# Turning B and C of two more pairs of chunks by VectorE: a state-space scan and an MLP on one core

## The chip, the core and the metric

The kernel runs on one core of a Trainium2 chip. A core has a matrix engine (TensorE, PE in the profile; PEld is its weight load), three engines for elementwise work (VectorE, DVE; ScalarE, ACT; GpSimd, POOL) and SyncE (SP), which here only issues transfers. Each engine works through its own queue of instructions in order and waits on semaphores for the others. Sixteen DMA engines move data between the memory (HBM) and the core's own memory (SBUF); TensorE writes its results to eight banks of PSUM. The metric is the device time of one execution in microseconds.

## The reference

Two blocks follow each other, all in float32 but for the weights, which arrive as float64.

The first is a state-space layer over 4 batches, 8 heads and 768 tokens, with a head width of 32 and a state width of 16. Per batch and head, in chunks of tokens:

```python
cum = cumsum(log(clip(a)))                       # inside the chunk
M = (C @ B.T) * exp(cum_i - cum_j) * causal      # tokens by tokens
y = M @ x + (C @ state) * exp(cum_i)
state = exp(cum_last) * state + (B * exp(cum_last - cum_j)).T @ x
```

The second is an MLP on the result, laid out as 3072 tokens by 256 (8 heads by 32):

```python
h = x @ w_in                                     # 256 -> 2048
g = maximum(h, 0) + alpha * minimum(h, 0)        # alpha per hidden unit
out = g @ w_out                                  # 2048 -> 256
```

## The kernel before

**Chunks, pairs, groups.** The kernel takes chunks of 128 tokens, 24 in all. Two neighbouring chunks of a batch are a pair (`gp`, 0 to 11); two pairs are a group of 512 tokens (0 to 5). A pair's state-space work gives 256 columns of xT, the input of the MLP in transposed form. While TensorE does the MLP of one group, the pairs of the next group are worked in between.

**Order.** There is no scheduler: the order of the program is the order on each engine. `first_two` does pairs 0 and 1. The loop `for f in range(FIRST, NF)` near the end does the MLP of group 0 (16 slices of 128 hidden units, steps 4 to 15 here) and spreads pairs 2 and 3 over it. From there on the loop over `quad` does the five other groups, in products of half the size combined as in Strassen's method, with the remaining pairs between them.

**A pair.** `load_pair` issues its transfers on SyncE's queue, `pair_loads` scales B with GpSimd (`bn`, line 533), and the generator `pair` does the rest in stages, each run by one call of `ssm`:
1. B and C of the pair are needed with the state's width on the partitions. Either TensorE transposes them against an identity (line 669, four 128x128 blocks into a PSUM tile from `ss_tile`) and ScalarE copies the result to SBUF (`bc`, line 672), or `turn_bc` has made `bc` before, with one VectorE transpose of 32x32 blocks (line 574). For this second way the rows must lie in SBUF so that every 32x32 block holds what is to be turned; the loads of lines 210 to 217 bring them in this form, in rows of 512 bytes (8 tokens by 16 numbers).
2. The new states (lines 629, 642, 645), C spread and decayed (lines 679, 682), and VectorE's scans of the decays (line 567), which read the tiles `abc`.
3. The products of B and C (line 742), times the decays (line 753, VectorE).
4. The products that give y (lines 797 and 805), and ScalarE's copy to xT (line 817).

Which way a pair goes is set in `load_pair` by `turned = gp > GC` with `GC = 4`: pairs 5 to 11 are turned by VectorE, pairs 2, 3 and 4 by TensorE (pairs 0 and 1 have a code of their own). A turned pair still loads B in its natural form, in rows of 64 bytes, since `bn` needs it; it doesn't load C so. `load_pair(2, ...)` is called with `parted=True` inside `first_two`: it loads chunk 0 of the pair and returns two functions for chunk 1, which are called some transfers later. `load_pair(3)` is issued at step 5, `load_pair(4)` at step 10.

**PSUM tiles.** While group 0 is in work, `ss_tile` deals its tiles in turn from a ring of two (`ss`) and one more bank (`bank(2)`), by a counter that every call moves on.

**Weights.** They come as float64 in pieces of 512 KB (`raw`; w_in and w_out by turns) and are made float32 by hand: ScalarE (lines 273, 283, 286), GpSimd (line 278), VectorE (sign and shift, lines 296 and 308), GpSimd again (line 330). The table `CONVERTED` says at which step a piece is converted. Group 0's MLP in line 1095 needs w_in, line 1142 needs w_out; ScalarE and VectorE apply the slopes between them (lines 1098 and 1099), and VectorE's line 1099 is the last to read the PSUM buffer `hp`, of which there are two. Sums of weights (line 1171) and of tokens (line 1183), which the other groups need, are GpSimd's.

```python
CONVERTED = {(4, 1): ("5", 5), (5, 1): ("6", 6), (6, 1): ("7",), (7, 0): ("8", 7), (7, 1): (8,),
```

Of the kernel before, what the change touches and what calls it, by code (L numbers as in the profile page):

```python
# [9 lines left out]
F32 = mybir.dt.float32  # L10
# [12 lines left out]
def kernel(  # L23
# [25 lines left out]
    nc = tc.nc  # L49
# [4 lines left out]
    batch, H, S, D = x.shape  # L54
    N = B.shape[-1]
    P = 128
    Q = 128
# [8 lines left out]
    GC = 4  # L66
# [9 lines left out]
    NB = 2  # L76
# [15 lines left out]
    work = ctx.enter_context(tc.tile_pool(name="work", bufs=2))  # L92
# [4 lines left out]
    gp = ctx.enter_context(tc.tile_pool(name="gp", bufs=16))  # L97
# [6 lines left out]
    def bank(i):  # L104


        return ps_q.tile([P, 512], F32, name="bank", tag=f"q{i}")
# [13 lines left out]
    loads = {}  # L121

    def load_rows(i, eng=nc.sync):

        rows = ld.tile([RW, Q], F32, name="rows")
        eng.dma_start(out=rows, in_=a.rearrange("b h (c t) -> (b h c) t", t=Q)[i * RW : (i + 1) * RW])
        loads["r", i] = rows
# [3 lines left out]
    def load_a(t, b, c, eng=nc.sync):  # L131
        first = a[b, 0:1, c * Q : (c + 2) * Q]
        eng.dma_start(out=t, in_=bass.AP(tensor=first.tensor, offset=first.offset,
                                             ap=[[S, H], [0, N], [1, 2 * Q]]))
# [4 lines left out]
    def load_tokens(dst, src, t0):  # L139


        d = dst.rearrange("p j (h w) -> p j h w", h=H)
        for k in range(2):
            for j in range(2):
                t = t0 + k * Q + j * HQ
                nc.sync.dma_start(out=d[HQ * k : HQ * (k + 1), j],
                                  in_=src[:, t : t + HQ, :].rearrange("h p w -> p h w"))
# [16 lines left out]
    def load_products(gp, ap):  # L164
        b, c = divmod(2 * gp, CPB)
        rows = scratch["pf", b // 2].rearrange("(b h c) t -> b h (c t)", b=2, h=H)
        rows = rows[b % 2, :, c * Q : (c + 2) * Q]
        nc.sync.dma_start(out=ap, in_=rows.unsqueeze(1).to_broadcast([H, N, 2 * Q]))

    def load_pair(gp, decays=True, parted=False):  # L170


        b, c = divmod(2 * gp, CPB)
        turned = gp > GC
        nat = ldx.tile([P, 3, 2, H * N], F32, name="nat")
        xt = ldx.tile([P, 2, HD], F32, name="xt")

        ap = ldx.tile([P, 2 * Q], F32, name="ap")
        if gp == 0:
            load_a(ap, b, c)  # L180
        elif gp > NB:
            load_products(gp, ap)
        if gp == 0:
            load_rows(0, nc.scalar)
        abc = []
        if gp >= HALF:
            load_tokens(nat[:, 0], B[b], c * Q)
        def load_bc(k):
            ts = slice((c + k) * Q, (c + k + 1) * Q)
            for i, src in enumerate((B,) if turned else (B, C)):  # L190
                eng = nc.scalar if gp == 0 and i else nc.sync
                eng.dma_start(out=nat[:, i, k].rearrange("p (h n) -> p h n", h=H),  # L192
                              in_=src[b, :, ts, :].rearrange("h p n -> p h n"))

        def load_x(k):
            ts = slice((c + k) * Q, (c + k + 1) * Q)
            nc.sync.dma_start(out=xt[:, k].rearrange("p (h d) -> p h d", h=H),  # L197
                              in_=x[b, :, ts, :].rearrange("h p d -> p h d"))

        for k in range((1 if parted else 2) if gp < HALF else 0):  # L200
            load_bc(k)
            if gp >= NB:
                load_x(k)
        for k in range(2 if gp < NB else 0):
            load_x(k)
        if gp == 0:
            nc.scalar.dma_start(out=al_n, in_=moe_alpha.rearrange("(k p) -> k p", p=P))
            loads["a", 1] = prep.tile([P, 2 * Q], F32, name="a1")
            load_a(loads["a", 1], b, c + 2)
        for i, src in enumerate((B, C) if turned else ()):  # L210


            for e in range(2):
                first = src[b, e : e + 1, c * Q : (c + 2) * Q, :]
                nc.sync.dma_start(out=nat[:, 1 + e, i],
                                  in_=bass.AP(tensor=first.tensor, offset=first.offset,
                                              ap=[[2 * S * N, P // 32], [8 * N, 32], [1, 8 * N]]))
        for k in range(2 if gp >= NB else 0):
            abc.append(lda.tile([P, H * Q], F32, name="abc"))
        loads["p", gp] = nat, abc, xt, ap  # L220
        if gp >= HALF:
            load_tokens(xt, x[b], c * Q)
        if decays:
            for part in load_spread(gp, b, c):
                pass
        return lambda: load_bc(1), lambda: load_x(1)

    def load_second():

# [116 lines left out]
    for v in range(2):  # L346
        vs = slice(HQ * v, HQ * (v + 1))
        nc.vector.tensor_copy(out=ident_q[vs].rearrange("p (c t) -> p c t", c=4),
                              in_=ident[vs, vs].unsqueeze(1).to_broadcast([HQ, 4, HQ]))
# [171 lines left out]
    def pair_loads(gp):  # L521

        b, c = divmod(2 * gp, CPB)
        nat, abc, xt, ap = loads["p", gp]

        bn = work.tile([P, 2, H * N], F32, name="bn")
        i, bi = divmod(b, 2)
        if gp >= HALF:
            pj = prt[i].rearrange("p (j b m h) -> p j b m h", j=2, b=2, h=H)[:, :, bi, c // 2]
        else:  # L530
            pj = (prt[i if gp >= NB else "short"]
                  .rearrange("p (b h c) -> p b c h", b=2, h=H)[:, bi, c : c + 2])
        nc.gpsimd.tensor_tensor(
            out=bn.rearrange("p k (h n) -> p k h n", h=H),
            in0=nat[:, 0].rearrange("p k (h n) -> p k h n", h=H),
            in1=pj.unsqueeze(3).to_broadcast([P, 2, H, N]), op=ALU.mult)
        return bn
# [12 lines left out]
    bcs = {}  # L550
# [3 lines left out]
    def scan_half(dec, abc, k, w):  # L554
# [10 lines left out]
        for i in range(2):  # L565
# [2 lines left out]
                                         data1=ident_p[0], initial=0.0, op0=ALU.mult,  # L568
                                         op1=ALU.add)

    def turn_bc(gp):

        bcs[gp] = work.tile([P, 4, Q], F32, name="bc")
        nc.vector.transpose(
            bcs[gp].rearrange("p (i k) t -> p i (k t)", i=2)
            .rearrange("p i (c b) -> p i b c", b=8),
            loads["p", gp][0][:, 1:].rearrange("p e i (b n) -> p (i b) e n", n=N))
        decs[gp] = work.tile([P, 2, H, Q], F32, name="dec")
        scan_half(decs[gp], loads["p", gp][1], 0, 0)

    def pair(gp):

        b, c = divmod(2 * gp, CPB)
        nat, abc, xt, ap = loads["p", gp]
        last = c + 2 == CPB
        fine = gp >= 2 * GC // 2
# [75 lines left out]


        bc = bcs.pop(gp, None)
        if bc is None:
            tp = ss_tile()
            for i in range(2):
                for k in range(2):
                    nc.tensor.transpose(tp[:, (2 * i + k) * P : (2 * i + k + 1) * P],
                                        nat[:, i, k], ident)  # L670
            bc = work.tile([P, 4, Q], F32, name="bc")
            nc.scalar.copy(out=bc.rearrange("p i t -> p (i t)"), in_=tp)
# [140 lines left out]
        for w in range(KC):  # L813
            if half:
                nc.scalar.copy(out=xts[g][:, :, (q + w) * Q : (q + w + 1) * Q], in_=y[w])
            if not half:
                nc.scalar.copy(out=xts[g][:, w, q * Q : (q + 2) * Q],
                               in_=y[w].rearrange("p k t -> p (k t)"))
# [317 lines left out]
    def output(f, half=None):  # L1136

        if f == 0:
            pos[0] = [bank(i).rearrange("p (t m) -> p t m", t=2) for i in range(GC // 2)]
        gt = gts[0, f]  # L1140
        for t in range(GC) if half is None else range(2 * half, 2 * half + 2):
            nc.tensor.matmul(pos[0][t // 2][:, t % 2], gt[:, t * Q : (t + 1) * Q], w_out[:, f],  # L1142
                             start=(f == 0 and t % 2 == 0), stop=(f == NF - 1),
                             skip_group_check=True)
# [309 lines left out]
    for f in range(FIRST, NF):  # L1454
        if f in (5, 10):
            load_pair(3 + f // 10)
        if f == 5:
            load_rows(1)
        hidden(0, f)
        for part in range(2):  # L1460
            if part:
                if f <= 10:
                    ssm(2)
                if f >= 9:
                    ssm(3)
            for i in CONVERTED.get((f, part), ()):
                if isinstance(i, str):
                    convert_a(*pieces[int(i)])
                else:
                    convert_next(first=False)  # L1470
        if f == 14:
            bns[4] = pair_loads(4)
            rows_clamp(1)
            held["pr"] = rows_scan(1)
            rows_out(1)
        if f == 8:
            bns[3] = pair_loads(3)
        output(f - FIRST)
        if f in in_steps:
            weight_sums(wi, in_sums, 0, in_steps[f])  # L1480
# [99 lines left out]
```

## Time and profile before

| what | value |
|---|---|
| runs | 356.65, 356.97, 358.07 us (median 356.97) |
| span of the profiled execution | 355.9 us |
| its own device time | not given beside the span; the median of the runs lies 1.07 us above it |
| TensorE busy | 349.3 us (98%), granted clock 1.000 |
| VectorE / ScalarE / GpSimd busy | 235.8 / 171.8 / 204.4 us |
| DMA | 105581 packets, 79896 of them under 512 bytes, 30.24 MB |
| DMA share in the second to fourth slice of 40 | 0.8 to 0.9 |
| line 669, transposes of pairs 2, 3, 4 | 12, 0.27 us each, at 29.0, 51.1 and 78.0 us |
| line 574, VectorE's turns of pairs 5 to 11 | 7, 1.11 us each |

How to read it: the span runs from the first to the last instruction. An engine's line in a timeline is start, length, engine, line of the kernel, operation, what is written from what, shape and count; in brackets the idle time before it and who ended that. SPq is SyncE's queue: the time that an issue took there, and not the transfer's. Neighbouring matmuls overlap, so what one costs is read from start to start. The DMA share is the mean busy share of the sixteen engines; it can pass 1 a little, since packets overlap.

### The profile page before, as it was taken

The page shows a single profiled execution, that of the slowest core. Times are in us where ns is not written, and L with a number is a line of the kernel's source. Part 1 is how long each engine was busy: PE and PEld are TensorE (multiplying, and loading weights), DVE is VectorE, ACT ScalarE, POOL GpSimd, SP SyncE. Part 2 cuts the span into 40 slices and gives each one's busy share as a digit, 9 for nine tenths or more (in the row PEclk, how much of TensorE's full clock was granted, in tenths as well). Part 3 has the DMA queues.
Part 4 walks back from the last instruction along what each step waited for, and adds up shares of the span by engine and source line. Part 5 has one row for each costly group of instructions (what it writes and reads, how often), then busy time and mean ns, then how long its engine had stood idle before and what let it go on. Part 6 is the DMA issues. An engine that isn't in the chain of part 4 may idle for free.

```text
span 355.9 us, 7778 instructions
## 1 busy us (share of the span) xinstructions
PE 349.3 (98%) x2985; PEld 284.4 (80%) x2985; DVE 235.8 (66%) x482; ACT 171.8 (48%) x391; POOL 204.4 (57%) x228
## 2 busy tenths in 40 slices
PE   8899999999999999999999999999999999999996
PEld 4576665578788888888888888888888888888885
DVE  6876986998748756847747856757856633643363
ACT  3477576535355346345345445345445344443431
POOL 6776568589939855725646626637526535434520
PEclk9999999999999999999999999999999999999999
DMA  7899989607345403503423423422001001001102
GB/s 138 182 202 270 329 174 279 148 17 159 106 83 128 102 3 75 104 2 77 78 57 74 86 51 71 85 55 65 11 2 31 0 2 29 2 1 31 31 0 59
DMA packets 105581, 30.24 MB, mean 85 GB/s; under 512 B 79896, under 2 KB 101448, under 8 KB 105544
## 3 DMA queue, kind: packets, MB, share of 16 engines
q1 hardware_dynamic: 103048, 29.43, 36.3%
q10 hardware_dynamic: 2496, 0.32, 0.6%
q8 instruction: 23, 0.38, 0.5%
q14 instruction: 14, 0.11, 0.1%
HBM read 26.32 MB, written 3.42 MB: 84 GB/s over the span
## 4 chain that ended last, share of the span: by engine, by line
PE 89%; SPq 4%; DMA 3%; DVE 2%; ACT 1%; POOL 1%; issue 0%; DVEq 0%; ACTq 0%
PE bank L1216 33%; PE hp L1241 29%; PE bank L1142 6%; PE ss L1241 6%; PE hp L1095 3%; DMA raw<-in_moe_w_in_dram 2%; SPq L192 2%; PE ss L787 1%; PE ss L731 1%; PE hp L1110 1%; PE bank L1209 1%; PE ss L805 1%; PE ss L779 1%; DMA xt<-in_x_dram 1%; SPq L197 1%; PE ss L742 1%
## 5 line engine op out<-in xcount | busy, mean ns | idle before, releaser
L1298 POOL TENSOR_TENSOR gt<-gt 128x512 f32<-128x512 f32 x58 | 74.2, 1279 | 21.1 <-DVE gt L1226 16.3
L1216 PE MATMUL bank<-gt,w_out 128*128 128x256 f32 x320 | 83.5, 381 | 0.0
L1216 PEld LDWEIGHTS bank<-gt,w_out 128*128 128x128 f32 x320 | 60.1, 190 | 9.2 <-issue 1.0
L1288 POOL TENSOR_TENSOR gt<-gt 128x512 f32<-128x512 f32 x20 | 25.4, 1269 | 62.5 <-DVE gt L1226 49.7
L1226 DVE SCALAR_TENSOR_TENSOR gt<-hp,s_mul,gt 128x256 f32<-128x256 f32 x96 | 42.0, 479 | 29.1 <-ACT gt L1224 26.8
L1224 ACT ACTIVATE gt<-hp,s_alpha 128x256 f32<-128x256 f32 x96 | 40.3, 471 | 34.5 <-PE hp L1241 31.4
L1216 PE MATMUL bank<-gt,ws 128*128 128x256 f32 x224 | 55.9, 379 | 0.0
L1216 PEld LDWEIGHTS bank<-gt,ws 128*128 128x128 f32 x224 | 42.3, 190 | 5.6
L1241 PE MATMUL hp<-xs,w_in 128*128 128x256 f32 x160 | 41.9, 384 | 0.0
L1241 PE MATMUL hp<-xs,ws 128*128 128x256 f32 x160 | 41.1, 380 | 0.0
L1267 DVE TENSOR_TENSOR hp<-hp,u 128x512 f32<-128x512 f32 x20 | 14.0, 700 | 35.2 <-ACT u L1265 35.2
L1241 PEld LDWEIGHTS hp<-xs,ws 128*128 128x128 f32 x160 | 30.3, 190 | 4.3 <-POOL xs L1183 0.2
L1241 PEld LDWEIGHTS hp<-xs,w_in 128*128 128x128 f32 x160 | 29.7, 190 | 4.5
L1142 PE MATMUL bank<-w_out,gt 128*128 128x256 f32 x128 | 31.1, 385 | 0.4 <-POOL w_out L330 0.4
L1142 PEld LDWEIGHTS bank<-w_out,gt 128*128 128x128 f32 x128 | 23.6, 190 | 7.2 <-issue 2.9
L1241 PE MATMUL ss<-xT,w_in 128*128 128x256 f32 x96 | 24.6, 379 | 0.0
L645 POOL TENSOR_TENSOR sm<-state,bmask 128x256 f32<-128x256 f32 (+1 forms) x10 | 6.2, 620 | 29.0 <-DVE state L642 29.0
L1095 PE MATMUL hp<-xT,w_in 128*128 128x512 f32 x48 | 22.8, 596 | 0.0
L561 DVE TENSOR_TENSOR_SCAN dec<-abc,bank 128x192 f32<-128x192 f32 x48 | 22.7, 522 | 0.0
L1256 ACT COPY m<-hp 128x512 f32<-128x512 f32 x8 | 4.7, 586 | 35.7 <-PE hp L1241 35.7
L1265 ACT COPY u<-hp 128x512 f32<-128x512 f32 x20 | 11.7, 585 | 19.4 <-PE hp L1241 19.4
L1226 DVE SCALAR_TENSOR_TENSOR gt<-c,s_mul,gt 128x256 f32<-128x256 f32 x40 | 20.6, 555 | 0.0
(232 smaller groups left out, 608.2 us busy)
## 6 DMA issues: line engine op xcount, KB each, us to landing
abc<-z SPq DMA_DIRECT2D x24, 192.0 KB
raw<-in_moe_w_in_dram SPq DMA_DIRECT2D x8, 512.0 KB
raw<-in_moe_w_out_dram SPq DMA_DIRECT2D x8, 512.0 KB
abc<-z SPq DMA_DIRECT2D x8, 512.0 KB
out_dram<-o_sb SPq DMA_DIRECT2D x32, 64.0 KB
nat<-in_B_dram SPq DMA_DIRECT2D x26, 64.0 KB
xt<-in_x_dram SPq DMA_DIRECT2D x12, 128.0 KB
xt<-in_x_dram SPq DMA_DIRECT2D x24, 64.0 KB
```

Of the source, the lines that this page charges most:

```text
L192: eng.dma_start(out=nat[:, i, k].rearrange("p (h n) -> p h n", h=H), in_=src[b, :, ts, :].rearrange("h p n -> p h n"))
L561: nc.vector.tensor_tensor_scan(out=dv[:, o : o + SQ], data0=abc[k][:, s : s + SQ], data1=ident_p[0][:, :SQ], initial=0.0, op0=ALU.mult, op ...
L1095: nc.tensor.matmul(hp, w_in[:, k, f * P : (f + 1) * P], xts[g][:, k], start=(k == 0), stop=(k == KC - 1))
L1142: nc.tensor.matmul(pos[0][t // 2][:, t % 2], gt[:, t * Q : (t + 1) * Q], w_out[:, f], start=(f == 0 and t % 2 == 0), stop=(f == NF - 1), s ...
L1216: nc.tensor.matmul(ms[g][i][:, h], w, blocks[g, z][n][:, p], start=(q == 0 and h == 0), stop=(q == NQ - 1), skip_group_check=True)
L1224: nc.scalar.mul(o[:, p], h[:, p], s_alpha[:, fs[p]])
L1226: nc.vector.scalar_tensor_tensor(out=o[:, p], in0=h[:, p], scalar=s_mul[:, fs[p]], in1=o[:, p], op0=ALU.mult, op1=ALU.max)
L1241: nc.tensor.matmul(to[:, p], w(2 * z + p), b, start=start and p == 0, stop=True, skip_group_check=True)
L1265: nc.scalar.copy(out=u2, in_=A)
L1267: nc.vector.tensor_tensor(out=Y, in0=Y, in1=u2, op=ALU.add)
L1288: nc.gpsimd.tensor_tensor(out=tc_, in0=g22, in1=g12, op=ALU.subtract)
L1298: eng.tensor_tensor(out=o, in0=x0, in1=x1, op=ALU.subtract)
```

## The change

Pairs 2 and 3 are now turned by VectorE as pairs 5 to 11 are. Their C is no longer loaded in its natural form, and TensorE's eight transposes, two PSUM tiles and ScalarE's two copies go. In their place come, for each of the two pairs, four loads of 64 KB in rows of 512 bytes (two of B, two of C) and one VectorE transpose.

For pair 2 the four loads are issued with the second part of its loads, after chunk 1's B. Its turn is made in `pair`, where the transposes were, in step 4 of group 0 and ahead of the conversions of that step. For pair 3 they follow its other B and x loads, and its turn is made at step 8, one step ahead of the first stage of that pair. Pair 4 stays as it was.

```diff
-        turned = gp > GC
+        turned = gp >= NB and gp != GC
...
-        for i, src in enumerate((B, C) if turned else ()):
-            for e in range(2):
-                first = src[b, e : e + 1, c * Q : (c + 2) * Q, :]
-                nc.sync.dma_start(out=nat[:, 1 + e, i], ...)
+        def load_blocks():
+            for i, src in enumerate((B, C)):
+                for e in range(2):
+                    first = src[b, e : e + 1, c * Q : (c + 2) * Q, :]
+                    nc.sync.dma_start(out=nat[:, 1 + e, i],
+                                      in_=bass.AP(tensor=first.tensor, offset=first.offset,
+                                                  ap=[[2 * S * N, P // 32], [8 * N, 32], [1, 8 * N]]))
+        if turned and not parted:
+            load_blocks()
...
-        return lambda: load_bc(1), lambda: load_x(1)
+        return lambda: (load_bc(1), load_blocks()), lambda: load_x(1)
...
-    def turn_bc(gp):
-        bcs[gp] = work.tile([P, 4, Q], F32, name="bc")
+    def turned_bc(gp):
+        bc = work.tile([P, 4, Q], F32, name="bc")
         nc.vector.transpose(
-            bcs[gp].rearrange("p (i k) t -> p i (k t)", i=2)
+            bc.rearrange("p (i k) t -> p i (k t)", i=2)
             .rearrange("p i (c b) -> p i b c", b=8),
             loads["p", gp][0][:, 1:].rearrange("p e i (b n) -> p (i b) e n", n=N))
+        return bc
+
+    def turn_bc(gp):
+        bcs[gp] = turned_bc(gp)
...
         bc = bcs.pop(gp, None)
+        if bc is None and not fine:
+            bc = turned_bc(gp)
...
         if f == 8:
             bns[3] = pair_loads(3)
+            bcs[3] = turned_bc(3)
```

(`fine` is true from pair 4 on; `NB` is 2.)

More of the change, by code (lines that the diff above doesn't have):

```diff
@@ L209, in load_pair @@
             load_a(loads["a", 1], b, c + 2)
-        for i, src in enumerate((B, C) if turned else ()):
-            for e in range(2):
-                first = src[b, e : e + 1, c * Q : (c + 2) * Q, :]
-                nc.sync.dma_start(out=nat[:, 1 + e, i],
-                                  in_=bass.AP(tensor=first.tensor, offset=first.offset,
-                                              ap=[[2 * S * N, P // 32], [8 * N, 32], [1, 8 * N]]))
+        def load_blocks():
[7 more added lines that the diff above has]
+            load_blocks()
         for k in range(2 if gp >= NB else 0):
```

## The prediction

> **What bounds the kernel now.** I read the page's busy times first, then TensorE's waits, then the chain that ended last, then the timelines of the stretch from 16 to 80 us, where every edited instruction lies.
>
> ```profile
> PE 349.3 (98%) x2985; PEld 284.4 (80%) x2985; DVE 235.8 (66%) x482; ACT 171.8 (48%) x391; POOL 204.4 (57%) x228
> ```
>
> TensorE is busy for 349.3 of 355.9 us. Of its listed waits only one lies after 22 us: 0.4 us for GpSimd's conversion of a piece of w_out (line 330). So a microsecond taken off TensorE's queue after 22 us shortens the run, as long as the others keep up. Where they nearly don't, the chain shows:
>
> ```profile
> 29.84 7.45 DMA raw<-in_moe_w_in_dram
> ...
> 38.13 0.83 POOL wt L278
> ...
> 38.98 0.69 DVE wr L308
> ...
> 44.52 1.28 POOL w_out L330
> ...
> 45.84 0.48 PE bank L1142
> ```
>
> A raw piece of w_in (the fifth, "in4") is issued at 29.84 and lands at 37.28. Its conversion goes through ScalarE, GpSimd and VectorE (38.98), VectorE then works without a gap to 44.43, GpSimd converts the next piece to 45.79, and TensorE, idle since 45.40, goes on. Two places before it are as tight: VectorE's line 1099 of step 6 ends at 40.33 and the products of line 742 start at 40.34 (0.10 after TensorE could); step 7's ends at 43.30 and line 1095 starts at 43.45, 2.00 after the group before it, where the same pair elsewhere takes 1.83 (33.25 to 35.08): 0.17. So from 40 to 46 us TensorE is tied to the landing of in4.
>
> The four transposes that go, with their neighbours, once for pair 2 and once for pair 3:
>
> ```profile
> 27.28 1.91 PE L1095 MATMUL hp<-xT,w_in 128*128 128x512 f32 x4
> 29.02 0.60 PE L669 MATMUL ss<-ident,nat 128*128 128x128 f32 x4
> 29.46 1.89 PE L1142 MATMUL bank<-w_out,gt 128*128 128x256 f32 x8
> ...
> 51.09 0.66 PE L669 MATMUL ss<-ident,nat 128*128 128x128 f32 x4
> 51.59 1.89 PE L1142 MATMUL bank<-w_out,gt 128*128 128x256 f32 x8
> ```
>
> VectorE's queue where the two new turns go, after the first line and before the third:
>
> ```profile
> 30.59 0.75 DVE L1099 SCALAR_TENSOR_TENSOR gt<-hp,s_mul,gt 128x512 f32<-128x512 f32 x1
> 32.51 0.43 DVE L296 TENSOR_SCALAR wr<-raw 128x512 uint32<-128x512 uint32 x1 [1.17 <-DMA raw<-in_moe_w_out_dram]
> ...
> 50.31 0.75 DVE L1099 SCALAR_TENSOR_TENSOR gt<-hp,s_mul,gt 128x512 f32<-128x512 f32 x1 [0.24 <-ACT gt L1098]
> ```
>
> And SyncE's queue, where a natural load of C is followed by an issue that must wait for room:
>
> ```profile
> 16.57 0.58 SPq L192 DMA_DIRECT2D nat<-in_C_dram  x1
> 17.19 2.19 SPq L197 DMA_DIRECT2D xt<-in_x_dram  x1
> ```
>
> **The change, part by part.**
>
> *TensorE* loses 4 + 4 transposes. Start to start they cost 29.46 - 29.02 = 0.44 (line 1095 before them takes its usual 1.72 to 1.74, so I take 0.46 against a start at 29.00) and 51.59 - 51.09 = 0.50.
>
> *ScalarE* loses the copies of bc (0.61 at 30.26, 0.58 at 51.78). After the first it idles 1.71, after the second it has work that GpSimd is late for anyway: nothing.
>
> *VectorE* gains two turns. The same form runs seven times later in this trace at 1.11 us (line 574). Pair 2's comes after line 1099 ends at 31.25 and before line 296 at 32.51, where VectorE idles 1.17 for the second piece of w_out ("out1"): it fills the gap, 31.3 to 32.4. Without that gap the cost would be 1.11 on the path. Queued behind it are the sign and shift of out1 (lines 296 and 308), for which GpSimd's line 330 waits. Pair 3's comes after the shift at 49.38, so at 50.07 to 51.2. Behind it: line 1099 of step 9 (0.9 late; its buffer is next needed at 57.3), line 296, and the shift at 52.28, needed by GpSimd at 54.84. From the end of the turn to the end of that shift there are 0.66 + 0.80 + 0.69 = 2.15 us of work, so the turn must have started by 54.84 - 2.15 - 1.11 = 51.5. At 50.07 it costs nothing; the cover is 1.4 us.
>
> *Bank rotation.* Without the two tiles for the transposes every later tile of these pairs moves to another bank. Each has been read by then (pair 3's second y goes to bank 2, whose next user is at 94.7): nothing.
>
> *SyncE's queue and the transfers.* Pair 2: two C loads go (0.58 each), four block loads come (two of B 1.17, two of C 1.12, by the pair at 82 us), all before "in3"; moved back by them are in3, the store of pf, x, out1, two abc, ap and in4. Pair 3: the same, with only abc, rows and late weights behind. GpSimd's queue keeps its order and its instructions. Two ends for in4:
> - Issue alone: 2.29 - 1.16 = 1.13 us later, if SyncE's waits stay.
> - Transfers alone: from 47 to 49 us C and x move 196 KB in 1.78 us of full share, 0.89 per 1024 packets. Out go 2 x 0.89. In come 4 x 64 KB in rows of 512 bytes; the nearest row is abc, also 512 bytes, 340 GB/s at a share of 1.09 (30 to 32 us), so 0.21 each. Net 1.78 - 0.84 = 0.94 earlier.
> The second is the nearer: the engines' share is about 1 from 29 to 43 us, and SyncE spends some 5 us from 17 to 26 waiting for room (2.19, 1.63, 1.82 and 1.56 against 0.5), which swallows 1.13. Between 19 and 22 us the share is only 0.73, 0.8 us unused behind the small packets; part of it should come back. I take 1.1 for in4 and out1. The other limit is VectorE itself: its gaps from 31.3 to 38.98 are 1.17, 1.05, 0.21 and 0.50; less the 1.11 of the turn, 1.8.
>
> One rule speaks against the edit. The Trainium skill, "DMA: Bandwidth & Descriptors", section Measured, gives 0.95 us for a transfer of 64 KB whatever its rows, and calls smaller ones descriptor-dominated. It was measured on another queue, and no row here times a block load alone. By it six small loads instead of four would add 2 x 0.95 = 1.9 us, and the sum would be about 1.5 us slower than before instead of the forecast below.
>
> A second, "VectorE: DVE Perf Modes", section Rules for kernel authors, sends 128x128 transposes to TensorE if the result may lie in PSUM. In busy time it fits the rows here (0.46 to 0.50 plus a copy of 0.6, against 1.11); by it the edit is a loss of next to nothing, but it doesn't ask which engine is full.
>
> **The sum.** Write e for how much earlier VectorE's shift at 38.98 comes. TensorE's ledger is 0.46 + (0.10 + 0.17 + 0.44) = 1.17 up to 45.84, but no more than e, then 0.50 at 51.1: at most 1.67. A second chain caps it. From 49.38 GpSimd and VectorE hand the conversions to each other with hardly a gap, and at 78.55 GpSimd starts the first token sum (line 1183), which ends at 79.28; TensorE uses it at 79.35, in a group of 0.95 where its like take 0.86. That chain moves by e, plus 0.27 (VectorE's wait at 68.25 for ScalarE, which waits for TensorE) plus 0.08. After it TensorE has no wait. So the gain is the least of 1.67, e + 0.50 and e + 0.35. With e = 1.1: 1.45. The profiled span becomes 355.9 - 1.45 = 354.45; the median of the runs stands 1.07 above the span, so 356.97 - 1.45 = 355.5 us.
>
> **The rivals.**
>
> *The weights land no earlier (e about 0).* For it: in4 lands 7.4 us after its issue, far more than its own 1.3 us, so what it waits for isn't all seen. Against it: the full shares. Then the first 1.17 are gone and the second chain leaves 0.35: 356.6. With e = -1.1, the other end, 0.75 slower: 357.7.
>
> *Slower: pair 3's rows land late and VectorE stands in its turn.* Place: the turn at 50.07. It decides from a start of 51.5; each microsecond beyond delays the conversions of 54.84 by one, and through line 1183 TensorE, less 0.35. If SyncE gains nothing, the last block is issued at about 47.7 + 2.3 = 50.0; pair 1's x landed 3.3 us after its issue, so 53.3: 358.4. With in4's 7.45 it would be 57.4 and 362.5. To be 0.5% slower the turn must start after 53.6. Against it: two loads of 1024 packets, each with up to 3.89 us of issue, are gone ahead of the blocks, and SyncE comes to them earlier.
>
> *More than the ledger.* Three groups of TensorE run 0.2 long beside their like (1.93 instead of 1.73, after line 742 and the rounds of pair 2); if these were hidden waits on the same chain, 0.4 to 0.6 more: 354.9 to 355.1. Against it: the same 1.93 recurs in places with nothing late.
>
> **How the numbers follow.** A difference of 0.5%, 1.8 us, is about what measurement can tell from no change here (runs 356.65 to 358.07). Forecast 0.56, own range 355.0 to 356.1; no earlier landing 0.17; late rows 0.17; more than the ledger 0.10. Faster by over 0.5% (under 355.18): the last and a quarter of the first, 0.24. Slower (over 358.76): three quarters of the late rows, 0.13. Else 0.63. The range of 354.8 to 358.2 leaves out a twentieth below and most of the late rows above.
>
> **What would show it.** No line 669 transposes before 70 us; two more turns of 1.11, the first without a wait at about 31.3; out1 and in4 landing about 1 us earlier; line 1142 after step 8 without its 0.4; line 1183's first at about 77.1; TensorE without a new wait. I'm wrong if VectorE waits in a turn, if in4 lands at 37.3 or later, or if TensorE waits in the 70s.

## The result, and the profile after

The changed kernel takes 358.06 us in the median of 20 runs (356.15 to 360.46), the kernel before on the same chip 356.59 us (20 runs, 355.82 to 358.07). The ratio is 1.0038, with a 95% interval of 1.0024 to 1.0051: slower, by 1.5 us where 1.45 us less had been forecast. It lies inside the range given and inside the 0.5% that was called hard to tell from nothing, but on the other side, and the forecast mechanism is not what decides it.

The busy times of the changed kernel, from the first part of the page:

```profile
PE 348.8 (98%) x2977; PEld 283.6 (80%) x2977; DVE 238.2 (67%) x484; ACT 171.2 (48%) x389; POOL 203.9 (57%) x228
```

The edit is there in full: eight TensorE transposes and two ScalarE copies fewer, two VectorE turns more. (Numbers of lines have moved: 278 is now 281, 286 is 289, 296 is 299, 308 is 311, 330 is 333, 533 is 536, 574 is 577, 1095 is 1105, 1099 is 1109, 1142 is 1152, 1171 is 1181, 1183 is 1193, 1241 is 1251.)

VectorE's timeline of the changed kernel at the two turns and behind the second (start, length, engine, line, operation, operands; in brackets the idle time before it and what ended that):

```profile
29.91 0.69 DVE L311 SCALAR_TENSOR_TENSOR wr<-wt,wr 128x512 uint32<-128x512 uint32 x1 [1.06 <-POOL wt L281]
30.58 0.75 DVE L1109 SCALAR_TENSOR_TENSOR gt<-hp,s_mul,gt 128x512 f32<-128x512 f32 x1
31.25 1.11 DVE L577 STREAM_TRANSPOSE bc<-nat 128x512 f32<-128x512 f32 x1
32.21 0.42 DVE L299 TENSOR_SCALAR wr<-raw 128x512 uint32<-128x512 uint32 x1
33.13 0.69 DVE L311 SCALAR_TENSOR_TENSOR wr<-wt,wr 128x512 uint32<-128x512 uint32 x1 [0.50 <-POOL wt L281]
...
50.61 1.13 DVE L577 STREAM_TRANSPOSE bc<-nat 128x512 f32<-128x512 f32 x1 [2.01 <-DMA nat<-in_C_dram]
51.59 0.68 DVE L1109 SCALAR_TENSOR_TENSOR gt<-hp,s_mul,gt 128x512 f32<-128x512 f32 x1
52.19 0.40 DVE L299 TENSOR_SCALAR wr<-raw 128x512 uint32<-128x512 uint32 x1
52.69 0.69 DVE L311 SCALAR_TENSOR_TENSOR wr<-wt,wr 128x512 uint32<-128x512 uint32 x1
53.30 1.50 DVE L299 TENSOR_SCALAR wr<-raw 128x512 uint32<-128x512 uint32 x1
56.67 0.69 DVE L311 SCALAR_TENSOR_TENSOR wr<-wt,wr 128x512 uint32<-128x512 uint32 x1 [1.86 <-POOL wt L281]
```

Pair 2's turn runs at 31.25 without a wait, as forecast. Pair 3's has VectorE standing for 2.01 us until the last block of C lands. GpSimd in the same stretch of the changed kernel:

```profile
50.80 0.65 POOL L536 TENSOR_TENSOR bn<-nat,prt 128x256 f32<-128x256 f32 x1
52.72 1.79 POOL L1181 TENSOR_TENSOR ws<-w_in 128x512 f32<-128x512 f32 x1 [1.28 <-ACT wg L289]
54.47 1.47 POOL L333 TENSOR_TENSOR w_in<-wr,wg 128x512 uint32<-128x512 uint32 x1
```

and of the kernel before:

```profile
52.33 1.14 POOL L533 TENSOR_TENSOR bn<-nat,prt 128x256 f32<-128x256 f32 x1
53.44 1.44 POOL L1171 TENSOR_TENSOR ws<-w_in 128x512 f32<-128x512 f32 x1
54.84 1.27 POOL L330 TENSOR_TENSOR w_in<-wr,wg 128x512 uint32<-128x512 uint32 x1
```

Before, the first weight sum (line 1171) starts the moment GpSimd is free. After, GpSimd idles 1.28 us ahead of it. The view names ScalarE, but the sum writes a tile of the pool that holds the raw weights (`wld`, tag `raw`), and the last reader of the piece whose buffer it takes is VectorE's sign at 52.19. In all five profiles with a late turn (below) the sum starts 0.13 to 0.14 us after that sign ends (here 52.59 and 52.72), and in one of them (`after_look_2`) ScalarE is not named. The sum then runs beside the shift at 52.69 and the next sign, and three instructions run longer than before: the sum 1.79 for 1.44, line 333 1.47 for 1.27, and the sign 1.50 for 0.87.

What TensorE makes of it, from its timeline in the changed kernel:

```profile
44.38 1.99 PE L1152 MATMUL bank<-w_out,gt 128*128 128x256 f32 x8 [0.44 <-POOL w_out L333]
...
65.34 1.98 PE L1105 MATMUL hp<-xT,w_in 128*128 128x512 f32 x4 [1.05 <-DVE gt L1109]
```

The old wait for w_out is still there, and at step 13 there is a new one of 1.05 us, which the kernel before does not have:

```profile
65.51 1.99 PE L1095 MATMUL hp<-xT,w_in 128*128 128x512 f32 x4
```

**Reading the two traces against each other.** Three points of a profile carry all that follows: the start of step 4 (TensorE's first line 1095 with 512 columns), VectorE's third shift of that stretch, "S" (line 308 at 38.98 before, line 311 at 37.52 after), and the start of the xs product (TensorE's first product with `xs`, line 1241, 79.35 and 79.17). Behind the xs product nothing differs: it ends the span 276.4 to 276.7 us later in all profiles of this study. A run's own time lies 1.7 to 1.8 us above its span (357.36 for 355.6 here). By that distance the first profile of before, with its span of 355.9, was of a run of about 357.65, one us above that kernel's median.

### The profile page after: what moved, and what is told of

Read it like the earlier page. It is cut to its first block, busy times and chain, and to the rows that moved or that the text cites. A ratio compares the mean times of both kernels' runs of the same rounds, so it can differ in the third digit from the quotient of the medians.

```text
span 355.6 us, 7765 instructions
## 1 busy us (share of the span) xinstructions
PE 348.8 (98%) x2977; PEld 283.6 (80%) x2977; DVE 238.2 (67%) x484; ACT 171.2 (48%) x389; POOL 203.9 (57%) x228
## 4 chain that ended last, share of the span: by engine, by line
PE 83%; DVE 5%; SPq 4%; POOL 2%; DMA 2%; issue 1%; ACT 1%; DVEq 0%; POOLq 0%
PE bank L1226 33%; PE hp L1251 29%; PE ss L1251 6%; PE bank L1152 4%; DVE dec L570 3%; PE hp L1105 2%; SPq L192 2%; DMA raw<-in_moe_w_in_dram 2%; PE ss L797 1%; PE ss L741 1%; DVE gt L1109 1%; PE hp L341 1%; PE bank L1219 1%; PE ss L789 1%; PE ss L815 1%
```

## The experiments

Each kernel ran beside the kernel before on the same chip. All profiles together first, sorted by what they show. Times are in microseconds from the start of each span; "from S" is the time from S to the xs product:

| kernel | step 4 | S | wait in pair 3's turn | xs product | from S | median us (runs) | ratio to before, 95% |
|---|---|---|---|---|---|---|---|
| before | 27.28 | 38.98 | - | 79.35 | 40.37 | 356.59 (20) | |
| before_again | 27.05 | 38.55 | - | 78.90 | 40.35 | 356.62 (10) | 1.0006, 0.9993 to 1.0019 |
| before_look_1 | 27.03 | 37.27 | - | 78.12 | 40.85 | 356.44 (1) | |
| before_look_2 | 27.15 | 37.65 | - | 78.25 | 40.60 | 356.57 (1) | |
| before_look_3 | 26.91 | 38.38 | - | 78.75 | 40.37 | 357.06 (1) | |
| pair2_only | 26.70 | 37.33 | - | 77.70 | 40.37 | 356.13 (12) | 0.9991, 0.9979 to 1.0003 |
| pair2_again | 26.94 | 37.20 | - | 77.59 | 40.39 | 356.24 (12) | 0.9990, 0.9973 to 1.0007 |
| pair2_blocks_later | 26.62 | 37.67 | - | 78.04 | 40.37 | 356.15 (12) | 0.9993, 0.9978 to 1.0007 |
| turn_in_gap | 27.20 | 38.37 | none | 78.74 | 40.37 | 356.72 (12) | 1.0002, 0.9982 to 1.0023 |
| blocks_first_gap | 26.48 | 38.28 | none | 78.65 | 40.37 | 356.73 (12) | 0.9998, 0.9977 to 1.0019 |
| blocks_first | 26.23 | 37.43 | none | 78.01 | 40.58 | 356.23 (12) | 1.0003, 0.9986 to 1.0019 |
| turn_other_rows | 26.96 | 37.90 | none | 78.48 | 40.58 | 356.65 (12) | 1.0003, 0.9990 to 1.0016 |
| other_rows_no_load | 27.00 | 37.88 | none | 78.44 | 40.56 | 356.64 (12) | 1.0012, 0.9995 to 1.0029 |
| after_look_1 | 26.44 | 37.94 | 1.48 | 79.08 | 41.14 | 357.28 (1) | |
| after_again | 26.52 | 37.82 | 1.77 | 79.23 | 41.41 | 358.64 (12) | 1.0047, 1.0024 to 1.0069 |
| after | 26.49 | 37.52 | 2.01 | 79.17 | 41.65 | 358.06 (20) | 1.0038, 1.0024 to 1.0051 |
| after_look_2 | 26.54 | 38.16 | 2.58 | 80.36 | 42.20 | 358.56 (1) | |
| pair3_only | 26.30 | 36.54 | 1.72 | 78.39 | 41.85 | 356.99 (12) | 1.0033, 1.0009 to 1.0057 |

### The two halves of the change, and the turn without its rows

`before_again` is the kernel before. `pair2_only`:

```diff
-        turned = gp >= NB and gp != GC
+        turned = gp == NB or gp > GC
...
-        if bc is None and not fine:
+        if bc is None and gp == NB:
...
-            bcs[3] = turned_bc(3)
```

`pair3_only` is the opposite half:

```diff
-        turned = gp >= NB and gp != GC
+        turned = gp == NB + 1 or gp > GC
...
-        return lambda: (load_bc(1), load_blocks()), lambda: load_x(1)
+        return lambda: load_bc(1), lambda: load_x(1)
...
-        if bc is None and not fine:
+        if bc is None and gp == NB + 1:
```

`turn_other_rows` turns pair 2's rows, long landed, a second time in place of pair 3's, so pair 3's products use pair 2's B and C; pair 3's own loads are still made:

```diff
-            bcs[3] = turned_bc(3)
+            bcs[3] = turned_bc(3, 2)
```

> The kernel before, unchanged, for a second profile. After the change the runs lie 1.76 us above their spans (357.36 against 355.6 in the profiled one). If that holds before it too, the first profile, with its span of 355.9, was a run of about 357.65, near the top of the 20 (355.82 to 358.07), and a usual span is 354.8. Both theories: ratio 1.000. If the first profile was an unusual one, the span is 354.5 to 355.2 now, and the fifth raw piece of weights lands earlier than 37.28 us; if it was usual, the span is 355.9 and the landing 37.3.

> Pair 2 alone is turned by VectorE, pair 3 by TensorE as before. Theory A (the loss is VectorE standing in pair 3's turn for late rows, 2.01 us in the profile): the gain of pair 2's part stays, 0.5 to 1.2 us, ratio 0.997 to 0.999. Theory B (the added loads of pair 2 delay the first weights in most runs): the loss is here, ratio 1.002 to 1.005.

> Pair 3 alone is turned by VectorE, at step 8; pair 2 by TensorE as before. Theory A: the whole loss without pair 2's gain, 1.5 to 3 us, ratio 1.004 to 1.008, VectorE waiting 0.5 to 2.5 us in the turn. Theory B: no loss, ratio 0.998 to 1.000.

> The changed kernel, but pair 3's turn reads pair 2's rows, which landed 20 us before; pair 3's own four loads are still made and nobody reads them. (Pair 3's products then use pair 2's B and C.) It takes the wait away and leaves all the work. Theory A: the loss goes and the forecast comes, ratio 0.995 to 0.998, no wait in the turn, TensorE without the 1.05 us at step 13. Theory C (the loss is the added transfers' load on the queue and on the weights behind them, or VectorE's 1.11 us itself): ratio stays at 1.003 to 1.005.

Pair 2 alone is level with before, not the 0.5 to 1.2 us faster that was expected. Pair 3 alone carries a loss (ratio 1.0033, expected 1.004 to 1.008), and without the wait for its rows the loss is gone: 356.65. The gain that was expected with it did not come. `before_again` has a span of 355.5, between the 354.5 to 355.2 expected of an unusual first profile and the 355.9 of a usual one, so two profiles did not decide that. In `pair3_only` the turn shows it once more:

```profile
49.83 1.12 DVE L577 STREAM_TRANSPOSE bc<-nat 128x512 f32<-128x512 f32 x1 [1.72 <-DMA nat<-in_C_dram]
```

So the loss belongs to the wait in pair 3's turn and not to the transfers of pair 2. That the two medians of the halves don't add up to the whole is within their intervals.

### Taking the wait away with the right rows, and taking the loads away

`blocks_first` issues pair 3's four block loads ahead of its B and x loads, in the same part of SyncE's queue:

```diff
+        if turned and not parted:
+            load_blocks()
         for k in range((1 if parted else 2) if gp < HALF else 0):
             load_bc(k)
...
-        if turned and not parted:
-            load_blocks()
```

`turn_in_gap` leaves the loads and makes the turn one step later:

```diff
                     convert_next(first=False)
+                if f == 9 and i == 10:
+                    turned_bc(3, to_turn.pop(3))
...
-            bcs[3] = turned_bc(3)
```

`other_rows_no_load` is `turn_other_rows` with `and gp != 3` at the block loads. `after_again` is the changed kernel.

> The changed kernel with pair 3's four block loads issued ahead of its B and x loads in the same part of SyncE's queue instead of behind them; the turn stays at step 8. Theory A: the rows land by about 47, before the turn is reached at 48.6; its wait of 2.01 us is gone, the turn costs its own 1.1 us against a cover of about 0.6, and the time is that of the turn on other rows, 356.4 to 356.9; stretch from step 4 to the xs product about 51.5. Theory B (the queue is starved of transfers between 45 and 50 whatever its order): what lands late is then x or B instead, the next raw weights land as late as before, and the time stays at 357.3 to 358.2.

> The changed kernel with pair 3's turn moved: it is issued after the shift (line 311) of step 9's conversions that VectorE makes at 52.7 in the changed kernel's profile and the sign (line 299) after it, that is into the stretch in which VectorE stood for 3.09 us before its shift at 55.2 when pair 3 was not turned at all. Pair 3's loads stay. Theory A (the loss is VectorE standing 2.01 us in the turn ahead of the sign that frees a raw buffer for GpSimd): the turn is then free, since its rows landed at 50.6; TensorE has no wait of about 1 us at step 13, the stretch from step 4 to the xs product is 50.6 to 51.2 (51.00 with pair 2 alone, less up to 0.5 for pair 3's transposes), and the time 355.7 to 356.3, below before by 0.3 to 0.9. Theory B (the transfers of pair 3 or the turn itself cost it, wherever it stands): stretch 51.6 to 52.7, time 356.7 to 358.

> The turn on pair 2's rows at step 8, as before, and pair 3's four block loads left out too (pair 3's B and C of the state sums are then pair 2's, so its outputs differ from the reference's). It tells the turn's own 1.1 us on VectorE from what its loads do to the other transfers. Theory A: the loads cost nothing beyond the rows' lateness, 356.4 to 356.8, within 0.2 of the same kernel with the loads (356.65). Theory B (the loads push back the raw weights, of which two more landed late): 355.8 to 356.2, about 0.5 less than with the loads.

> The changed kernel once more, on the same chip as the three others, to have a second profile and a time beside theirs. If the wait in pair 3's turn carries the loss, its profile shows it again at 1.5 to 2.5 us, with TensorE's wait of about 1 us for line 1109 at step 13 behind it, and the time is 357.3 to 358.2. If the first profile's wait was a chance of that execution, it is below 1 us and the stretch from step 4 to the xs product below 52.

On one chip, beside 356.32 of before: 356.23 and 356.72 with the wait removed in the two ways, 356.64 without the loads, and 358.64 for the changed kernel (above the 357.3 to 358.2 expected). The wait is shown as the cause. The loads themselves cost nothing that can be seen (356.64 without, 356.65 with them, on two chips with 356.32 and 356.44 of before). The expectation of 355.7 to 356.3 for the turn in the gap was missed: with the wait gone the kernel is level with before, and not 0.3 to 0.9 faster. VectorE at the turn in `blocks_first`:

```profile
48.43 1.15 DVE L577 STREAM_TRANSPOSE bc<-nat 128x512 f32<-128x512 f32 x1
...
50.94 0.69 DVE L311 SCALAR_TENSOR_TENSOR wr<-wt,wr 128x512 uint32<-128x512 uint32 x1 [0.51 <-POOL wt L281]
...
55.50 0.69 DVE L311 SCALAR_TENSOR_TENSOR wr<-wt,wr 128x512 uint32<-128x512 uint32 x1 [3.09 <-POOL wt L281]
```

VectorE's idle stretch ahead of its later shift (3.08 us at 56.84 in the kernel before) is back with 3.09; where the turn waits only 1.86 are left.

Where the rows' lateness comes from, in the DMA columns (the last two: share of the sixteen engines, GB/s) of the stretch 45 to 48 us, of the changed kernel

```profile
45.00:48.00 3.00, 3.00 (x11) 1.62 (x9) 2.90 (x6) 2.40 (x5) 1.90 (x2) 1.00 0.40 93
```

and of `blocks_first`

```profile
45.00:48.00 3.00, 3.00 (x18) 1.61 (x24) 2.90 (x6) 2.33 (x5) 1.89 (x2) 1.00 0.88 136
```

In the changed kernel SyncE's queue reaches the blocks late, behind two B and two x loads. The second B, the second x and the blocks:

```profile
39.79 3.19 SPq L192 DMA_DIRECT2D nat<-in_B_dram  x1
43.03 0.90 SPq L197 DMA_DIRECT2D xt<-in_x_dram  x1
43.97 1.18 SPq L215 DMA_DIRECT2D nat<-in_B_dram  x2
45.20 1.12 SPq L215 DMA_DIRECT2D nat<-in_C_dram  x2
```

The last block's issue ends at 46.32 and its rows are there at 50.61, 4.3 us later. The low share from 45 to 48 us is mostly that of the block loads themselves, as two kernels that differ in these four loads alone show: `turn_other_rows`, with them, and `other_rows_no_load`, without,

```profile
45.00:48.00 3.00, 3.00 (x12) 1.95 (x11) 2.91 (x5) 2.82 (x6) 1.90 (x2) 1.00 0.51 98
45.00:48.00 3.00, 3.00 (x12) 1.94 (x11) 2.92 (x5) 2.87 (x6) 1.89 (x2) 1.00 1.03 250
```

and in the changed kernel one stretch inside it stays near a quarter of the engines:

```profile
46.00:47.00 1.00, 1.00 (x4) 0.56 (x3) 1.00 (x3) 1.00 (x3) 0.92 (x2) 1.00 0.26 77
48.00:49.00 1.00, 1.00 (x49) 0.79 (x52) 0.60 (x1) 0.69 (x1) 0.25 (x1) 1.00 1.09 322
```

At 77 GB/s 64 KB take 0.85 us (an estimate from the first row), and four loads 3.4, where the prediction had 0.84 for all four. So the rows come late for two reasons: the loads are reached late, and they are slow. 0.26 is about what four of sixteen engines would show, and the outermost dimension of these loads' source is 4 (`P // 32`); that this sets the pace is likely, but no run changed the form, so it is not shown. In the kernel before the stretch is low too (0.54 busy, 68 GB/s from 45 to 48), with other loads and nothing on the path waiting for it; that was not settled.

### Both repairs, and what differs between executions

`blocks_first_gap` has both edits above. `pair2_blocks_later` is `pair2_only` with the blocks behind the next raw weights:

```diff
-        return lambda: (load_bc(1), load_blocks()), lambda: load_x(1)
+        return lambda: load_bc(1), lambda: load_x(1), load_blocks
...
         load_bc()
         load_next()
+        load_blocks()
```

`after_look_1` and `after_look_2` are single profiles of the changed kernel.

> Both repairs together: pair 3's blocks issued ahead of its B and x loads, and its turn put into VectorE's idle stretch of step 9. Theory C, formed from the runs so far: the xs product starts a fixed 40.37 us after VectorE's shift near 38 us (40.35 to 40.37 in both profiles of before, with pair 2 alone and with the turn in the gap; 40.56 to 40.58 with a turn at step 8 that does not wait; 41.41 to 41.85 with one that waits), and the 276.5 us behind it do not move. Then this kernel has 40.35 to 40.40 and no wait in either turn; as pair 3's rows can't come late any more its runs lie at 355.7 to 356.6 in the median, with none above 358.5, and it is not faster than pair 2 alone, though TensorE has 0.5 us less to do. If TensorE's work were what sets the end, it would be 0.5 faster than pair 2 alone, 355.3 to 355.7.

> Pair 2 alone turned by VectorE, its four block loads issued behind the next raw weights in SyncE's queue instead of ahead of them; pair 3 stays with TensorE. If the blocks hold that raw load back (it landed at 28.4 with VectorE's shift waiting 1.06 for GpSimd in the changed kernel), the load lands 0.5 to 1 us earlier against step 4's start, the shift near 38 comes 0.2 to 0.6 earlier against it than with pair 2 alone (10.6 us behind step 4's start there) and the time is 355.5 to 356.0. If raw weights are held by the transfers of the first 24 us as a whole, it stays at 356.0 to 356.4. The blocks are then needed at 31: should they land late, VectorE waits in pair 2's turn and the time goes to 356.5 to 357.5.

> One more profile of the changed kernel, whose runs reach from 356.2 to 360.5, to see what differs between its executions. If the wait in pair 3's turn is what differs, the stretch from the shift near 38 to the xs product (41.65 and 41.41 in two profiles, with waits of 2.01 and 1.77) grows by as much as the wait, and the 276.5 us behind it stay. If a longer execution shows the same wait and stretch, the spread comes from the first 38 us or from behind the xs product.

> As the look before it: the wait in pair 3's turn and the stretch to the xs product grow together, or neither does and the spread is elsewhere.

Neither beats before. `blocks_first_gap` (356.73, just above the 355.7 to 356.6 expected) has its 40.37 and no wait, and TensorE's time for pair 3's transposes is worth nothing there. Moving pair 2's blocks back changed nothing either (356.15 against 356.13).

The two profiles show how the wait counts. In the longer execution, 358.56 us, VectorE's lines are

```profile
51.82 1.11 DVE L577 STREAM_TRANSPOSE bc<-nat 128x512 f32<-128x512 f32 x1 [2.58 <-DMA nat<-in_C_dram]
...
53.38 0.40 DVE L299 TENSOR_SCALAR wr<-raw 128x512 uint32<-128x512 uint32 x1
```

and GpSimd's

```profile
53.92 1.79 POOL L1181 TENSOR_TENSOR ws<-w_in 128x512 f32<-128x512 f32 x1 [1.84 <-issue]
55.68 1.44 POOL L333 TENSOR_TENSOR w_in<-wr,wg 128x512 uint32<-128x512 uint32 x1
```

From the start of the late turn to the xs product it is 28.57, 28.56, 28.56, 28.54 and 28.56 us in the five profiles with a wait (`after_look_1`: 79.08 - 50.51; `after_again`: 79.23 - 50.67; `after`: 79.17 - 50.61; `after_look_2`: 80.36 - 51.82; `pair3_only`: 78.39 - 49.83). So from S + 12.6 to 13.7, where these five turns start, each microsecond of lateness is one microsecond of time. Carried back to 40.37, that line begins at S + 11.8 (40.37 - 28.56); no profile has a turn that starts between S + 11.0 and S + 12.6, so this point is an estimate.

The longest executions were not profiled. Runs of 359.0 us or more: 11 of 46 in the kernels that wait in pair 3's turn (`after`, `after_again`, `after_look_1`, `after_look_2`, `pair3_only`), none of 106 in the other kernels tried here, one of the 130 timed of before beside them. That they are later rows again is likely from this, and not shown. Two of the eleven ran at a granted clock of 0.995, at which the sixteen runs on record take 357.5 to 359.1 us; the other nine ran at 0.998 to 1.000.

### Whether pair 2's part advances S

> One more profile of the kernel before. Its two profiles have VectorE's shift near 38 at 38.98 and 38.55, and their own runs were 357.65 (by 1.75 above the span) and 357.24, above the median of 356.4. By the fixed 40.37 to the xs product, 276.5 behind it and 1.75 around the span, a run of 356.4 must have the shift at 37.8. If so, the shift comes no later here than with pair 2 turned (37.33 to 38.37 in ten profiles), and the part of pair 2 gives nothing. If the shift is at 38.5 to 39.0 again, pair 2's part gives about 0.9 there and the run is 357.2 to 357.7.

> As the look before it. Whatever the time of the shift, it is followed by 40.35 to 40.37 us to the xs product and 276.5 us behind that.

> As the two looks before it: a shift at 37.3 to 38.3 means that pair 2's part advances nothing, one at 38.5 to 39.0 that it advances about 0.9.

> Pair 2 alone once more, on the same chip as the looks at the kernel before, for its time and a second profile. If pair 2's part advances the shift by 0.9, as between the profiles so far, the median is 355.4 to 355.7; if the shift of the kernel before is usually as early, it is 356.0 to 356.4, as in its first runs (356.13).

S in the five profiles of before: 38.98, 38.55, 37.27, 37.65, 38.38, in the mean 38.17. In the twelve profiles with pair 2 turned it goes from 37.20 to 38.37, in the mean 37.79. The two sets overlap, and `pair3_only`, which does not turn pair 2, had 36.54. The profile that the forecast was made from had the latest of all. It had VectorE idle 1.17 us for the second piece of w_out; the three later profiles of before do not have that. VectorE in `before_look_1`:

```profile
30.34 0.75 DVE L1099 SCALAR_TENSOR_TENSOR gt<-hp,s_mul,gt 128x512 f32<-128x512 f32 x1
31.01 1.44 DVE L296 TENSOR_SCALAR wr<-raw 128x512 uint32<-128x512 uint32 x1
32.95 0.69 DVE L308 SCALAR_TENSOR_TENSOR wr<-wt,wr 128x512 uint32<-128x512 uint32 x1 [0.51 <-POOL wt L278]
```

The expectation that 40.35 to 40.37 always follow S fell: `before_look_1` and `before_look_2` have 40.85 and 40.60. There S came early and TensorE's own work was the bound, 51.09 and 51.10 us from step 4 to the xs product (78.12 - 27.03, 78.25 - 27.15). In all five profiles of before the xs product starts, within 0.03 us, at the later of step 4 + 51.09 and S + 40.37. (Both constants are taken from these profiles; 40.37 holds in four kernels with pair 2 turned as well.) So the chain of VectorE and GpSimd is one of two bounds, and TensorE the other. With 0.46 less for TensorE a kernel with pair 2 turned has step 4 + 50.63: 77.57 for `pair2_again`, and 77.57 by S, measured 77.59. So pair 2's part lets TensorE be some 0.45 faster (50.65 us from step 4 to the xs product there, against the 51.09 that no profile of before goes below), and what of that shows depends on S of the execution. The medians of the three kernels with pair 2 alone lie 0.2 to 0.3 us below before, each with an interval that holds 1. A gain there is likely and not shown.

## Why the prediction was wrong

**TensorE as the bound, and the ledger of 1.67.** The terms of the removed transposes were right: steps 4 to 5 take 3.47 us instead of 3.91 (26.49 to 29.96 against 27.28 to 31.19), 0.44 for the 0.46 named, and from step 9 to 10 it is 5.25 instead of 5.64 (46.21 to 51.46, 47.67 to 53.31), 0.39 for the 0.50. What failed is the step from there to the run's time. In the two profiles of before nearest its median the two bounds lie 0.2 and 0.5 us apart (`before_look_2`: 78.24 by TensorE, 78.02 by S; `before_look_1`: 78.12 and 77.64), so what is taken off TensorE beyond that leaves the other. Pair 3's part is worth nothing in any profile here.

**The term e = 1.1.** "I take 1.1 for in4 and out1" was mis-sized. Against the first profile S did come 1.46 us earlier (37.52), and the conversions of out1 and in4 began at 30.45 and 35.75 instead of 32.57 and 37.37. But `before_look_1` has S at 37.27 without any change. Between the means of the profiles S comes 0.4 us earlier with pair 2 turned, less than the spread of either set. The 1.17 us of idle VectorE that pair 2's turn was to fill are there in two of the five profiles of before (1.17 and, in `before_again`, 1.15) and in none of the other three. The turn is free all the same, for a reason not foreseen (last section): the sign behind it, 1.44 us long in `before_look_1`, takes 0.42 after the turn. From line 1099 to the shift behind that sign it is 2.61 us in `before_look_1` (30.34 to 32.95) without the turn and 2.55 in `after` (30.58 to 33.13) with it.

**"The second chain caps it", e + 0.35.** Right that there is such a chain, up to line 1183; wrong in where it begins and in its slack. It begins at S, not at 49.38, and where it binds the 0.27 and 0.08 are no gain: 40.37 with and without pair 3's transposes.

**"At 50.07 it costs nothing; the cover is 1.4 us."** This is the step that made the result. Two things in it failed.
- The start: the turn was reached in time (S + 11.0 in `blocks_first` and `turn_other_rows`, forecast 50.07 - 38.98 = 11.09), but the rows were not there. The last blocks were issued earlier than the rival allowed for (45.4 to 47.9, not 50.0), landed 3.9 to 4.4 us after that (not 3.3), and the turn began at S + 12.6 to 13.7. The sum had taken a block load's price from abc, "so 0.21 each"; at the 77 GB/s measured while they are in work it is 0.85, four times as much.
- The cover: I asked when the shift behind the turn is needed (54.84) and overlooked that GpSimd's first weight sum takes the buffer that the sign behind the turn sets free. In `after` the sum starts at S + 15.20 instead of S + 14.46, 0.74 late; then it and line 333 run 0.35 and 0.20 us longer. Together 1.29, against 41.65 - 40.37 = 1.28 measured. So the turn had to start by about S + 11.8, which with the first profile's S is 50.8, and the cover was some 0.7 us and not 1.4.

**The turn's own cost.** Without a wait 0.2 us (40.56 to 40.58 instead of 40.37), about what GpSimd's line 281 beside it grew (0.87 in `blocks_first` for 0.67 in `turn_in_gap`); one step later nothing. VectorE had the room.

**The rival that came true.** "Pair 3's rows land late and VectorE stands in its turn" was the mechanism, given 0.17 and 358.4 to 362.5 us; measured 358.06, just below that. Its price, one for one, was right, without the 0.35 that it took off. Its point of decision was some 0.7 us too late, and what was held against it ("SyncE comes to them earlier") is true but not enough.

**The offset.** The sum was set against a span of 355.9 and a median of 356.97, 1.07 apart. The distance of a run to its span is 1.7 to 1.8 in every run here, so the profile was of an execution some 0.7 us above the three runs' median, 1.1 above that of twenty. The gaps it showed were partly its own.

**What was to show it.** No line 669 before 70 us, two turns of 1.11, the first at 31.3 without a wait: so it was. Line 1142 after step 8 without its 0.4: no, 0.44. Line 1183's first at 77.1: no, 78.36. TensorE without a new wait: no, 1.05 at step 13. "I'm wrong if VectorE waits in a turn": it did, 2.01 us.

**The two rules.** The Trainium skill, "DMA: Bandwidth & Descriptors", section Measured, was weighed as an estimate: 0.95 us for each load of 64 KB, 1.5 us slower. (Its table goes by size alone and does not speak of rows.) The sign of that sum matched, its mechanism not: without pair 3's four loads the time is the same (356.64 and 356.65). For the load itself the 0.85 us estimated above is near that figure. "VectorE: DVE Perf Modes", section Rules for kernel authors, sends 128x128 transposes to TensorE. For pair 3 these runs come out that way, for a reason of this kernel: TensorE's transposes were hidden, and VectorE's turn, of 32x32 blocks, costs 0.2 us where it stood, more where its rows are late. For pair 2 they don't: VectorE's turn is free.

## What to carry to other kernels

An instruction moved onto an in-order engine brings its inputs' landing times with it: ask when its rows land, not only whether the engine has room, and issue its loads ahead of those that nobody waits for. Take the price of such a load from a row of the same form, not only of the same row length. The deadline behind such a wait is the earliest of all consumers, and a buffer handed on through a pool (here from a raw weight to a weight sum) is one of them. Before a gap in a profile is spent, see whether that execution was a typical one: compare its own time, not its span, with the median, and take a second profile if they differ.

## What the runs showed of the hardware

- A 128x512 sign on VectorE (uint32, one operand) takes 0.40 to 0.43 us when GpSimd is idle as it starts (`after`, 52.19). When a GpSimd operation is in work, with at least 0.12 us still to go, the sign ends 0.27 to 0.30 us after that operation does, however long that takes: all 144 such signs between 20 and 90 us in the eighteen profiles do so, and the 108 others take 0.40 to 0.43. In `before_look_1` GpSimd's line 330 runs from 30.89 to 32.16, and the sign begun at 31.01 ends at 32.45 (1.44 us); in `after` the weight sum ends at 54.51, and the sign begun at 53.30 ends at 54.80 (1.50 us). VectorE's transpose takes 1.10 to 1.15 in every place here, also while GpSimd's line 333 runs its usual 1.28 beside it (`after`, 31.06 to 32.34). So in pair 2's place the transpose fills time in which the sign would have been slow.
- Four loads of 64 KB in rows of 512 bytes, queued behind loads in rows of 64 and 128 bytes, land 3.9 to 4.4 us after the last issue; while they are in work the sixteen engines are 0.26 busy at 77 GB/s (`after`, 46 to 47 us), and without them the stretch from 45 to 48 us is 1.03 busy at 250 GB/s (`other_rows_no_load`). Issued ahead of those loads they are there in time, and the stretch is 0.88 busy (`blocks_first`).
- The start of step 4 lies between 26.23 and 27.28 us from one execution to the next, in kernels whose instructions up to there are the same too (26.30 in `pair3_only`, 26.91 to 27.28 in before). What sets it was not looked for. From there to the xs product the five profiles of before take 51.09 to 52.07 us, the spread that S explains, and behind it all profiles 276.4 to 276.7.
